# A seventh table of pairs and short slots for experts' last tokens

## The chip, the cores and the metric

The kernel runs on one core of one Trainium2 chip. The metric is the device time in microseconds (us) of one execution. The names PE, DVE, ACT, POOL and SP stand for the engines TensorE, VectorE, ScalarE, GpSimd and SyncE.

## What is computed

The reference has two halves. The first is a long convolution by Fourier transform, whose result multiplies the input; it gives 45824 rows (tokens) of 128 numbers. The second is a mixture of experts over these rows:

```
skip_score = x @ w_skip;  do_compute = skip_score > 0
out = x.copy();  xc = x[do_compute]
logits = xc @ w_gate                 # 8 experts
e_idx = argmax(logits);  gate_w = softmax(logits)[e_idx]
for e in range(8):                   # F = 1024
    h = relu(xc[e_idx == e] @ w1[e])            # 128 -> 1024
    y[e_idx == e] = gate_w * (h @ w2[e])        # 1024 -> 128
out[do_compute] = xc + y
```

The inputs are drawn with a fixed seed. Counted with the reference, 22861 tokens are computed, and the eight experts get 2546, 2933, 2278, 3602, 2666, 2440, 2962 and 3434 of them. In blocks of 256 that is 93 blocks, the last of each expert partly filled: with 242, 117, 230, 18, 106, 136, 146 and 106 tokens.

## The kernel before, in words

Three stages run one after the other: the first transforms and the filter (to about 350 us), the product in frequency and the way back (to about 900 us), and the output stage, which makes the rows, routes each token to its expert and stores all rows to memory. The output stage works in 32 chunks of 128 x 12 rows. For each chunk it appends the tokens' row numbers to lists, one list per expert.

An expert's tokens are computed in **slots** of 256 (`T`). A **table** decides which experts' blocks fill the next slots. `KNOWN` lists the tables: `(c, n, u)` says that after chunk `c` a table fills `n` units of `u` slots each. With `u` = 2, a **pair**, both slots belong to one expert, so that they share its weights. Before, six tables give 72 slots. The first 28 (`NEARLY`) run beside the output stage (`early_slots`), 44 as 22 pairs after it. A table after the last chunk (`last`) gives `NLAST` = 21 single slots. What is left over runs in a loop whose count is known at run time only (L919; it starts at `NLAST`). `table` (L535) is a generator: its small DVE operations and small PE products on 8 numbers are spread over the steps of the output stage, at two points of each step (`tabled`).

The code of each step is written in a fixed order, and each engine takes its instructions in that order. The early slots are a second generator (`work`): one piece of it goes into each step, and `PACE` - 1 more pieces per step on average. What remains of it follows the last step.

`late_slots` (L802) then goes through its units `u`. For a unit it gathers the rows four units ahead (`fetch`, L643 on POOL, one indirect DMA for 128 rows), turns them (PE transposes into `mtp`, L695), splits them and the weights into a high and a low part (L697 and L701, L678 and L683), and makes each product as three fp32r products (L706 to L708 for the first product `up`, L839 to L841 for `down`). ACT and DVE take the first product through relu as a high and a low part (L827, L828). The down product has the 128 features on the partitions, so its result is copied (`yt`, L845, once per unit, on ACT), transposed back (`mto`, L852), weighted and added on DVE (L719) and stored by POOL (L712, one indirect DMA for 128 rows). After each unit's gathers and after its stores POOL writes a small tile (`idle`, L616). The down product of unit `u` - 1 stands between the up products of unit `u`.

Of the kernel before, what the change touches and what calls it, by code (L numbers as in the profile page):

```python
# [39 lines left out]

KNOWN = ((3, 4, 1), (5, 4, 1), (9, 3, 2), (14, 7, 2), (23, 12, 2), (29, 10, 2))
SOON = 4
# [6 lines left out]
QX = 4  # L49
PACE = 1.3  # L50
START = (0, 4, 7)
# [7 lines left out]
FETCH = 4  # L59
NLATE = 65  # L60
NLAST = NEARLY + NLATE - NKNOWN
NTAB = 188
IDLE = 512
FRONT = 7


def units():

    at, found = 0, []
    for n, u in [(n, u) for _, n, u in KNOWN] + [(NLAST, 1)]:  # L70
        found += [list(range(k, k + u)) for k in range(at, at + n * u, u)]
        at += n * u
    return [v for v in found if v[0] < NEARLY], [v for v in found if v[0] >= NEARLY]

# [406 lines left out]
class Experts:  # L481
# [7 lines left out]
    def __init__(self, tc, i, out, lists, mc, wf):  # L489
# [28 lines left out]
        nc.vector.memset(self.found, 0.0)  # L518
        self.tab = mc.tile([1, NKNOWN + NTAB], I32, name="tab")
        self.addr = mc.tile([1, NKNOWN + NTAB], I32, name="addr")  # L520
        self.total = mc.tile([1, 1], I32, name="total")
        self.ids = mc.tile([128, NKNOWN + NLAST, 2], I32, name="ids")
        self.flat = lists.rearrange("a b -> (a b)")
# [10 lines left out]

    def table(self, last, base, limit, unit, pool, ps):  # L535

# [3 lines left out]
        mm = nc.tensor.matmul  # L540
        col = lambda name, dt=F32: pool.tile([E, 1], dt, name=name)
        shift, incl = self.shift[:, 0], self.shift[:, 1]
        done, iota = self.done, self.iota[:, 0:limit]
        ni, nt, cum, step = col("tni", I32), col("tnt", F16), col("tcum"), col("tstep")
# [16 lines left out]

        past = pool.tile([E, NTAB], F32, name="past", bufs=1)[:, 0:limit]
        pasth = pool.tile([E, NTAB], F16, name="tph", bufs=1)[:, 0:limit]
        nc.vector.tensor_scalar(past, iota, cum, None, ALU.is_ge)
# [6 lines left out]
        yield  # L571
        at = pool.tile([1, NTAB], F32, name="trow", bufs=1)[:, 0:limit]
        nc.vector.scalar_tensor_tensor(at, iota[0:1], float(T * unit), r, ALU.mult, ALU.add)
# [5 lines left out]
        if not last:  # L579

            dn = col("tdn")
# [20 lines left out]
    def fetch(self, at, ids, since):  # L602
        at = self.nc.sync.value_load(at, min_val=0, max_val=END)
        ins = self.nc.sync.dma_start(ids, self.flat[ds(at, T)].rearrange("(p a) -> p a", a=2))
        self.group(ins, "fetches", *(f"list{c}" for c in self.listed if c > since))

    def issue(self, s, ch):
        self.fetch(self.addr[:, s:s + 1], self.ids[:, s], ch)

# [192 lines left out]
    def late_slots(self, pool):  # L802
# [4 lines left out]
        with (  # L807
# [40 lines left out]
            def leave(sts, yt):  # L848
# [9 lines left out]
                self.rest()  # L858

            self.apart = False  # L860
            st, w, h = self.ahead
# [3 lines left out]
            def fetch(u):  # L865
                if u < count:
                    for n in UNITS[u]:
                        if n not in st:
                            st[n] = self.gather(n, self.ids[:, n], pool, self.names[n])
# [4 lines left out]
            sts = lambda u: [st[n] for n in UNITS[u]]  # L874
            w2, yt = {}, {}
            before = iter(())
            for u in range(count + 2):
                fetch(u + FETCH)
                if u + 1 < count:
                    hl[u + 1] = turned(sts(u + 1))  # L880

                def first():
                    if u + 1 < count:
                        w1[u + 1] = self.split(st[UNITS[u + 1][0]][0], pool, 0, nc.vector)
# [4 lines left out]
                def finish():  # L889
                    if u >= 2:  # L890
                        leave(sts(u - 2), yt.pop(u - 2))

                def lower():
                    y = next(before, None)
                    if y is not None:
                        yt[u - 1] = y
                parts = []
                if u >= count:
                    finish()
                elif len(UNITS[u]) == 1:  # L900
                    first()
                    hp = up(w1[u], hl[u], 0)
                    finish()
                    parts.append(relu(hp))
                    second()
                    parts.append(relu(up(w1[u], hl[u], 1)))
                else:
                    for k, rest in enumerate((finish, first, second, lambda: None)):
                        hp = up(w1[u], hl[u], k)
                        lower()  # L910
                        parts.append(relu(hp))
                        rest()
                while u >= 1 and u - 1 < count and u - 1 not in yt:
                    lower()
                if u < count:
                    before = down(w2[u], parts, hl[u].shape[2])
                    del w1[u], hl[u]
# [37 lines left out]
def out_phase(tc, i, out, zd, ex, consts):  # L955
# [6 lines left out]
    with (  # L962
        tc.tile_pool(name="slot", bufs=2, reuse_waits="tile") as eb,
    ):
      with (
# [237 lines left out]
        groups = [(s, ch, b) for ch, (b, n, u) in checks.items() for s in range(b, b + n * u)]  # L1203
        groups += [(s, NCH - 1, NKNOWN) for s in range(NKNOWN, NKNOWN + NLAST)]
        fresh = []

# [25 lines left out]
        def routed(ch):  # L1232
            route(ch)
            last = ch == NCH - 1
            if last or ch in checks:
                span = (NKNOWN, NTAB, 1) if last else checks[ch]
                tables.append(ex.table(last, *span, ob, tabs))

# [139 lines left out]
```

## Time and profile before

| | us |
|---|---|
| median of 3 runs | 1631.91 |
| the three runs | 1627.84, 1638.36, 1631.91 |
| the profiled execution's own time | 1634.26 |
| its span, first to last instruction | 1632.5 |

The profile is of one execution. Over the whole span PE is busy for 95%, DVE for 73%, POOL for 67% and ACT for 49%; PE alone holds 79% of the chain of work that ended last. The output stage ends near 1213 us; from there to the end only expert slots run. Lines (L845) are those of the kernel before; in the changed kernel the same lines stand 14 to 70 further down. Matmuls overlap one another in the records, so the distance from one start to the next is the time that one takes.

### The profile page before, as it was taken

The numbers are of one execution on the slowest core, as the hardware profiler recorded it, in microseconds if no ns is written. First come the engines' busy times: TensorE is split into PE (matmuls) and PEld (weight loads), VectorE is DVE, ScalarE is ACT, GpSimd is POOL, SyncE is SP. The second block draws the span as 40 slices with busy tenths as digits, with TensorE's granted clock in tenths as the row PEclk, the third lists the DMA queues.
The fourth block names the chain that finished last, engine by engine and source line by source line (L and its number), as shares of the span: only waits on it lengthen the run. The fifth ranks groups of instructions, "written<-read, shape, count | busy, mean of one in ns | idle before, by whom it ended". The sixth has DMA issues, their size and how long they took to land.

```text
span 1632.5 us, 26515 instructions
## 1 busy us (share of the span) xinstructions
PE 1542.9 (95%) x8272; PEld 965.3 (59%) x8272; DVE 1198.7 (73%) x2403; ACT 795.1 (49%) x1691; POOL 1099.1 (67%) x857
## 2 busy tenths in 40 slices
PE   8976999999999999988889999999989999998997
PEld 3542444444444444433467766666778877888997
DVE  2325877888788799985878777777867776776886
ACT  5543545445444444433344453443545554555764
POOL 1103898888988788850474749656687876766885
PEclk9897999999999999999899999999999999999999
DMA  9998999999999789969967778769321111111110
GB/s 324 325 340 313 383 378 377 352 331 317 341 338 330 246 263 334 290 195 338 308 207 241 252 237 244 244 213 286 104 43 42 44 45 39 44 35 35 34 34 21
DMA packets 200644, 361.92 MB, mean 222 GB/s; under 512 B 64842, under 2 KB 141018, under 8 KB 200462
## 3 DMA queue, kind: packets, MB, share of 16 engines
q1 hardware_dynamic: 181078, 316.98, 57.3%
q0 software_dynamic: 16704, 38.89, 8.4%
q10 hardware_dynamic: 2720, 4.34, 0.9%
q8 instruction: 67, 1.10, 0.3%
q14 instruction: 75, 0.61, 0.1%
HBM read 216.96 MB, written 145.69 MB: 222 GB/s over the span
## 4 chain that ended last, share of the span: by engine, by line
PE 79%; DVE 7%; issue 6%; DMA 4%; ACT 1%; POOL 1%; SPq 0%; another core or an unknown queue 0%; DVEq 0%; ACTq 0%; POOLq 0%
PE ps L405 19%; PE xp L374 12%; PE bank L789 6%; PE ps L203 4%; PE y L1031 4%; PE hp L706 4%; PE hp L708 4%; PE my L841 4%; PE my L839 4%; PE my L840 4%; PE hp L707 4%; PE tp L1044 2%; PE mh L706 2%; PE bank L1052 1%; DMA x1f<-fx 1%
## 5 line engine op out<-in xcount | busy, mean ns | idle before, releaser
L405 PE MATMUL ps<-y,c 128*128 128x512 f32 x720 | 331.3, 597 | 0.3
L472 POOL TENSOR_TENSOR y<-y,p 128x2048 f32<-128x2048 f32 x59 | 267.6, 4535 | 68.7 <-DVE p L394 68.7
L712 POOL DMA_INDIRECT out<-o,ids x186 | 205.5, 1105 | 151.1 <-DVE o L719 110.6
L405 PEld LDWEIGHTS ps<-y,c 128*128 128x128 f32 x720 | 133.4, 190 | 173.0 <-issue 155.7
L643 POOL DMA_INDIRECT xt<-out,ids x186 | 197.4, 1061 | 50.8 <-issue 32.5
L394 DVE TENSOR_TENSOR p<-xp,g 128x1024 f32<-128x1024 f32 x240 | 217.4, 948 | 0.0
L828 DVE SCALAR_TENSOR_TENSOR hh<-hp,hh 128x1024 fp32r<-128x1024 f32 x130 | 158.4, 1218 | 76.5 <-ACT hh L827 47.5
L394 DVE TENSOR_TENSOR y<-xp,g 128x1536 f32<-128x1536 f32 x120 | 210.8, 1757 | 4.0
L406 ACT COPY z<-ps 128x512 f32<-128x512 f32 x180 | 105.5, 586 | 178.5 <-PE ps L405 164.5
L827 ACT ACTIVATE hh<-hp 128x1024 fp32r<-128x1024 f32 x130 | 134.2, 1032 | 86.7 <-PE hp L708 52.0
L473 POOL TENSOR_TENSOR y<-y,p 128x1024 f32<-128x1024 f32 x59 | 139.0, 2356 | 4.6
L683 DVE TENSOR_TENSOR ws<-wf,ws 128x1024 fp32r<-128x1024 f32 x104 | 126.6, 1217 | 12.7 <-ACT ws L678 9.9
L616 POOL MEMSET idle<- 128x512 f16 x248 | 134.5, 542 | 0.2
L706 PE MATMUL hp<-hl,ws 128*128 128x512 f32 (+1 forms) x344 | 124.4, 362 | 7.5 <-DVE hh L828 5.2
L203 PE MATMUL ps<-wf,c 60*120 60x384 f32 x512 | 113.4, 535 | 12.1 <-DVE wf L186 11.4
L1031 PE MATMUL y<-zt,c 128*64 128x512 f32 x384 | 110.9, 647 | 14.0 <-DVE xm L1032 8.0
L789 PEld LDWEIGHTS bank<-wd,h 128*128 128x128 f32 x896 | 105.5, 194 | 29.6 <-issue 29.6
L374 PE MATMUL xp<-x,wf 128*128 128x480 f32 x256 | 115.5, 575 | 7.3 <-issue 3.5
L205 ACT COPY wf<-ps 120x384 f32<-120x384 f32 x256 | 105.6, 493 | 26.7 <-PE ps L203 25.9
L707 PE MATMUL hp<-hl,ws 128*128 128x512 f32 (+1 forms) x344 | 116.7, 339 | 1.0 <-issue 1.0
L841 PE MATMUL my<-hh,ws 128*128 128x512 f32 (+1 forms) x344 | 117.2, 341 | 0.4 <-issue 0.4
L839 PE MATMUL my<-hh,ws 128*128 128x512 f32 (+1 forms) x344 | 117.2, 341 | 0.0
(165 smaller groups left out, 3003.5 us busy)
## 6 DMA issues: line engine op xcount, KB each, us to landing
wf<-xv SPq DMA_DIRECT2D x64, 768.0 KB
x1d<-wf SPq DMA_DIRECT2D x64, 720.0 KB
x<-x1d SPq DMA_DIRECT2D x60, 768.0 KB
zt<-zd SPq DMA_DIRECT2D x60, 768.0 KB
zd<-z SPq DMA_DIRECT2D x110, 384.0 KB
out<-xm SPq DMA_DIRECT2D x96, 258.0 KB
ox<-xo SPq DMA_DIRECT2D x96, 256.0 KB
x1f<-fx POOLq DMA_DIRECT2D x16, 720.0 KB
```

The costliest lines, as they stand in the source:

```text
L203: nc.tensor.matmul(ps[p], self.c1[rows], u[rows, q * RUN:(q + 1) * RUN], start=True, stop=True)
L374: nc.tensor.matmul(xp[:, k, 0:(NS + NB) * DH], c2(n % PER * KS + j * KH + k), x1[:, j * KH + k], start=True, stop=True)
L394: nc.vector.tensor_tensor(o[:, :, :, j * KH:(j + 1) * KH].rearrange("p s a k b d -> p (s a) k b d"), x[:, None].broadcast_to([128, m, KH, ...
L405: nc.tensor.matmul(zps, c3[:, a, :], y[:, blk, a], start=(a == 0), stop=(a == 1))
L472: nc.gpsimd.tensor_tensor(y[:, 1:], y[:, 1:], p1, ALU.add)
L643: ins = nc.gpsimd.indirect_dma_start(out=xt[:, j], out_offset=None, in_=self.rows[0:have], in_offset=bass.IndirectOffsetOnAxis(ap=ids[:, j ...
L706: nc.tensor.matmul(hp, w[:, 0, c], hl[:, 0], start=True, stop=False)
L707: nc.tensor.matmul(hp, w[:, 0, c], hl[:, 1], start=False, stop=False)
L712: ins = nc.gpsimd.indirect_dma_start(out=self.rows, out_offset=bass.IndirectOffsetOnAxis(ap=ids[:, j:j + 1], axis=0), in_=o, in_offset=Non ...
L789: nc.tensor.matmul(bank[:, j * D:(j + 1) * D], h[f][:, j * 128:(j + 1) * 128], wd[s][:, f * D:(f + 1) * D], start=(f == 0), stop=(f == F / ...
L839: nc.tensor.matmul(y, w2[:, 0, c], h[:, 0], start=(f == 0), stop=False)
L841: nc.tensor.matmul(y, w2[:, 1, c], h[:, 0], start=False, stop=(f == F // 128 - 1))
```

## The change

The seven steps of it: a table of 7 pairs after chunk 32 is added to `KNOWN`; `NLAST` falls from 21 to 3 (28 + 61 - 86); four short slots (`NHALF`) are added at the end; the last table of pairs counts a block as full when it holds more than 128 tokens (`most`); a new table (`half`) finds the experts whose last block has 1 to 128 tokens and takes that block out of `found`; `PACE` goes from 1.3 to 1.24; and `late_slots` gets a short form for the short slots. That form gathers 128 rows, transposes once, copies the weights once instead of splitting them, uses one plain fp32 product instead of three fp32r ones, does relu on ACT alone, and makes the down product with the tokens on the partitions, so that `yt` and the transpose back fall away.

```
-KNOWN = ((3, 4, 1), (5, 4, 1), (9, 3, 2), (14, 7, 2), (23, 12, 2), (29, 10, 2))
+KNOWN = ((3, 4, 1), (5, 4, 1), (9, 3, 2), (14, 7, 2), (23, 12, 2), (29, 10, 2), (32, 7, 2))
-PACE = 1.3
+PACE = 1.24
-NLATE = 65
+NLATE = 61
+NHALF = 4
+HALF = NKNOWN + NTAB
...
+    found += [[HALF + k] for k in range(NHALF)]
...
-    def table(self, last, base, limit, unit, pool, ps):
+    def table(self, kind, base, limit, unit, pool, ps):
...
+        half, last = kind == "half", kind == "last"
...
-        nc.vector.tensor_scalar(ni, self.found, float(T - 1 if last else 0), None, ALU.add)
-        nc.vector.tensor_scalar(ni, ni, 8, None, ALU.arith_shift_right)
+        def rounded(n, up):
+            nc.vector.tensor_scalar(n, self.found, float(up), None, ALU.add)
+            nc.vector.tensor_scalar(n, n, 8, None, ALU.arith_shift_right)
+        rounded(ni, {"full": 0, "most": T // 2 - 1, "half": T - 1, "last": T - 1}[kind])
+        if half:
+            done, nw = col("done", F16), col("nw", I32)
+            rounded(nw, T // 2 - 1)
+            nc.vector.tensor_copy(done, nw)
...
-            nc.vector.scalar_tensor_tensor(done, dn, float(unit), done, ALU.mult, ALU.add)
+            if half:
+                nc.vector.scalar_tensor_tensor(self.found, dn, float(-T), self.found, ALU.mult, ALU.add)
+            else:
+                nc.vector.scalar_tensor_tensor(done, dn, float(unit), done, ALU.mult, ALU.add)
...
-        for j in range(2):
+        for j in range(ids.shape[1]):
...
+            def turned_half(st):
+                tp = mpt.tile([128, 2 * T], F32, name="mtp")[:, 0:128]
+                nc.tensor.transpose(tp, st[1][:, 0, 0:D], self.ident)
+                x = pool.tile([128, 2, 2 * T], F32R, name="hl", bufs=2)[:, 0, 0:128].bitcast(F32)
+                nc.scalar.copy(x, tp)
+                return x
+
+            def weight_half(st, which, p, eng):
+                w = p.tile([128, 2, F], F32R, name=f"ws{which}", bufs=2)[:, 0].bitcast(F32)
+                src = (self.w1f, self.w2f)[which][:, ds(self.where(eng, st[0]), F)]
+                (eng.copy if eng is nc.scalar else eng.tensor_copy)(w, src)
+                return w
+
+            def up_half(w, x):
+                hp = mph.tile([128, 4 * T], F32, name="hp")
+                for f in range(F // 128):
+                    c = slice(f * 128, (f + 1) * 128)
+                    nc.tensor.matmul(hp[:, c], w[:, c], x, start=True, stop=True)
+                h = mb.tile([128, 2, 4 * T], F32R, name="hh", bufs=6)[:, 0].bitcast(F32)
+                nc.scalar.activation(h, hp, AF.Relu)
+                return h
+
+            def down_half(w, h):
+
+                y = mpy.tile([128, 2 * T], F32, name="my")[:, 0:D]
+                for f in range(F // 128):
+                    c = slice(f * 128, (f + 1) * 128)
+                    nc.tensor.matmul(y, h[:, c], w[:, c], start=(f == 0), stop=(f == F // 128 - 1))
+                yield y
+
+            def leave_half(st, y):
+                tb, xt, ids, since = st
+                o = self.row()
+                self.gated(o[:, 0, 0:D], y, xt, 0)
+                self.store(o[:, 0], ids, 0)
+                self.rest()
...
-                tables.append(ex.table(last, *span, ob, tabs))
+            if not last and ch in checks:
+                tables.append(ex.table("full", *checks[ch], ob, tabs))
+            if last:
+                tables.append(zip_longest(ex.table("most", *checks[ch], ob, tabs), ex.table("half", HALF, NHALF, 1, ob, tabs[:, 64:])))
+                tables.append(ex.table("last", NKNOWN, NTAB, 1, ob, tabs))
```

How the order of the instructions moves is shown at three places. The first is DVE after the last chunk's counts are in `found`. Before, three small operations of the table `last` follow `tf` (the tokens' places in their lists), and then the weighting of an early pair:

```order
L1158 CAST tf<-to 128x24
L545 TENSOR_SCALAR tni<-found 8x1
L546 TENSOR_SCALAR tni<-tni 8x1
L548 TENSOR_TENSOR tnt<-tni,done 8x1
L719 SCALAR_TENSOR_TENSOR o_4455<-bank_4479,xt_4451 128x128 x2
```

Now the tables `most` (t...) and `half` (h...) open with eleven:

```order
L1228 CAST tf<-to 128x24
L554 TENSOR_SCALAR tni<-found 8x1
L555 TENSOR_SCALAR tni<-tni 8x1
L564 TENSOR_TENSOR tni<-tni,done 8x1
L565 TENSOR_SCALAR tni<-tni 8x1
L566 CAST tnt<-tni 8x1
L554 TENSOR_SCALAR hni<-found 8x1
L555 TENSOR_SCALAR hni<-hni 8x1
L554 TENSOR_SCALAR hnw<-found 8x1
L555 TENSOR_SCALAR hnw<-hnw 8x1
L560 CAST hdone<-hnw 8x1
L562 TENSOR_TENSOR hnt<-hni,hdone 8x1
```

PE's first products of the table (on `tnt`, now also on `hnt`) wait for the last of them. The second place is PE a little later, where the table `last` now runs as a third one behind the other two, between groups of eight products of an early pair (L810, L789 before):

```order
L810 MATMUL bank_4479<-wd,h 128x128 x8
L568 LDWEIGHTS shift
L568 MATMUL bank_4478<-tnt,shift 8x1
L569 LDWEIGHTS shift
L569 MATMUL bank_4478<-done,shift 8x1
L810 MATMUL bank_4479<-wd,h 128x128 x8
L582 LDWEIGHTS onesf
L582 MATMUL bank_4478<-tph,onesf 1x188
L583 MATMUL bank_4478<-tpast,tstep 1x188
L584 LDWEIGHTS done
L584 MATMUL bank_4478<-first,done 1x188
L810 MATMUL bank_4479<-wd,h 128x128 x8
```

Before, this part of the program had one table with its products between pieces of early work, and no second one behind it. The third place is PE at the very end, in the short slots (`xt_4448` and `xt_4449` are the rows of the last two, `mto` belongs to the last single slot):

```order
L883 MATMUL mtp<-ident,xt_4448 128x128
L898 MATMUL hp<-hl,ws_17864 128x128 x8
L908 MATMUL my<-ws_17853,hh 128x128 x8
L873 MATMUL mto<-ident,yt 128x128 x2
L883 MATMUL mtp<-ident,xt_4449 128x128
L898 MATMUL hp<-hl,ws_17940 128x128 x8
L908 MATMUL my<-ws_17929,hh 128x128 x8
L898 MATMUL hp<-hl,ws_18003 128x128 x8
L908 MATMUL my<-ws_17992,hh 128x128 x8
L908 MATMUL my<-ws_18039,hh 128x128 x8
```

Where a single slot had 48 products of 256 columns and four transposes, a short one has 16 products of 128 columns and one transpose.

## Rows read from the trace of the kernel before

**Rows 1.** The head of the page.
```profile
span 1632.5 us, 26515 instructions
```

**Rows 2.** Windows: output stage, its end, pairs, single slots; busy us of each engine.
```profile
core 0: us, PE busy (x) PEld busy (x) DVE busy (x) ACT busy (x) POOL busy (x), PEclk, DMA share, GB/s
900.00:1150.00 250.00, 245.85 (x2057) 168.15 (x2055) 194.28 (x687) 114.23 (x286) 164.34 (x194) 1.00 0.78 247
1150.00:1213.00 63.00, 57.57 (x457) 45.72 (x455) 44.57 (x171) 25.26 (x52) 45.69 (x54) 0.97 0.26 64
1213.00:1484.00 271.00, 264.14 (x1239) 216.77 (x1240) 195.41 (x280) 152.34 (x179) 203.07 (x213) 0.99 0.16 41
1484.00:1622.00 138.00, 131.70 (x1066) 129.29 (x1064) 111.09 (x157) 89.89 (x119) 105.73 (x113) 0.98 0.12 31
```

**Rows 3.** Timeline of ACT, the copy that ends a unit: start us, us, line.
```profile
1228.60 0.58 ACT L845 COPY yt<-my 128x512 f32<-128x512 f32 x1 [2.13 <-PE my L841]
...
1450.48 0.59 ACT L845 COPY yt<-my 128x512 f32<-128x512 f32 x1 [2.12 <-PE my L841]
1462.30 0.59 ACT L845 COPY yt<-my 128x512 f32<-128x512 f32 x1 [2.12 <-PE my L841]
...
1490.42 0.37 ACT L845 COPY yt<-my 128x256 f32<-128x256 f32 x1 [1.58 <-issue]
...
1606.35 0.37 ACT L845 COPY yt<-my 128x256 f32<-128x256 f32 x1 [1.53 <-PE my L841]
1612.53 0.38 ACT L845 COPY yt<-my 128x256 f32<-128x256 f32 x1 [1.52 <-PE my L841]
1618.49 0.37 ACT L845 COPY yt<-my 128x256 f32<-128x256 f32 x1 [1.69 <-PE my L841]
1622.31 0.37 ACT L845 COPY yt<-my 128x256 f32<-128x256 f32 x1 [3.45 <-issue]
```

**Rows 4.** Timeline of ACT, 1369 us: a late start within the pairs.
```profile
1369.34 1.02 ACT L827 ACTIVATE hh<-hp 128x1024 fp32r<-128x1024 f32 x1 [5.18 <-PE hp L708]
```

**Rows 5.** Timeline of PE: plain fp32 products of 128 columns, 64 together.
```profile
1202.21 7.31 PE L789 MATMUL bank<-wd,h 128*128 128x128 f32 x64
```

**Rows 6.** Lines, each form apart, 1213 to 1622 us: busy us, mean ns.
```profile
L712 POOL DMA_INDIRECT out<-o,ids x130 | 146.7, 1128 | 72.5 <-DVE o L719 42.0 <-issue 25.0 <-DVE hh L828 2.1
L827 ACT ACTIVATE hh<-hp 128x1024 fp32r<-128x1024 f32 x129 | 133.1, 1032 | 80.2 <-PE hp L708 45.5 <-issue 20.6 <-PE mtp L695 5.6
...
L683 DVE TENSOR_TENSOR ws<-wf,ws 128x1024 fp32r<-128x1024 f32 x85 | 103.4, 1217 | 11.4 <-ACT ws L678 9.9 <-DVE hl L701 0.8 <-issue 0.7
L678 ACT CAST ws<-wf 128x1024 fp32r x85 | 88.5, 1042 | 2.9 <-issue 2.3
...
L616 POOL MEMSET idle<- 128x512 f16 x85 | 46.1, 543 | 0.0
L719 DVE SCALAR_TENSOR_TENSOR o<-mto,xt 128x128 f32<-128x128 f32 x128 | 36.5, 337 | 4.8 <-PE hp L708 2.8 <-PE mto L852 1.9
```

**Rows 7.** The same view of the whole run: a copy of 128 columns on ACT.
```profile
L1054 ACT COPY lt<-bank 128x128 f32<-128x128 f32 x96 | 26.0, 271 | 21.7 <-PE bank L1052 19.9 <-PE bank L1144 0.5
```

**Rows 8.** Timeline of POOL at the end.
```profile
1623.84 0.97 POOL L712 DMA_INDIRECT out<-o,ids  x1 [1.03 <-DVE o L719]
1625.12 0.97 POOL L712 DMA_INDIRECT out<-o,ids  x1 [0.30 <-issue]
1626.09 0.54 POOL L616 MEMSET idle<- 128x512 f16 x1
```

**Rows 9.** Timeline of DVE: ten small operations of a table, first and last.
```profile
1164.38 0.15 DVE L573 SCALAR_TENSOR_TENSOR trow<-iota,bank 1x10 f32<-1x10 f32 x1
...
1165.58 0.15 DVE L586 SCALAR_TENSOR_TENSOR done<-tdn,done 8x1 f16<-8x1 f32 x1
```

**Rows 10.** Windows: ten us near the end of the output stage.
```profile
1180.00:1190.00 10.00, 7.34 (x65) 6.86 (x64) 8.63 (x30) 0.96 (x4) 6.84 (x8) 0.89 0.43 107
```

**Rows 11.** Waits of PE, 1150 to 1213 us: us in total, times, longest.
```profile
PE bank L1121 <- DVE ct L1112: 2.1, 1, 2.1
```

More of the change, by code (lines that the diff above doesn't have):

```diff
@@ L1 @@
+from itertools import zip_longest
 import numpy as np
@@ L518, in __init__ @@
         nc.vector.memset(self.found, 0.0)
-        self.tab = mc.tile([1, NKNOWN + NTAB], I32, name="tab")
-        self.addr = mc.tile([1, NKNOWN + NTAB], I32, name="addr")
+        self.tab = mc.tile([1, HALF + NHALF], I32, name="tab")
+        self.addr = mc.tile([1, HALF + NHALF], I32, name="addr")
         self.total = mc.tile([1, 1], I32, name="total")
-        self.ids = mc.tile([128, NKNOWN + NLAST, 2], I32, name="ids")
+        self.ids = mc.tile([128, NKNOWN + NLAST + NHALF, 2], I32, name="ids")
         self.flat = lists.rearrange("a b -> (a b)")
@@ L533, in weights @@
                           i["moe_w2"][e].rearrange("(c p) d -> p c d", p=128))
-    def table(self, last, base, limit, unit, pool, ps):
+    def table(self, kind, base, limit, unit, pool, ps):
         nc = self.nc
         mm = nc.tensor.matmul
-        col = lambda name, dt=F32: pool.tile([E, 1], dt, name=name)
+        half, last = kind == "half", kind == "last"
+        pre, room = ("h", limit) if half else ("t", NTAB)
+        col = lambda name, dt=F32: pool.tile([E, 1], dt, name=pre + name)
         shift, incl = self.shift[:, 0], self.shift[:, 1]
         done, iota = self.done, self.iota[:, 0:limit]
-        ni, nt, cum, step = col("tni", I32), col("tnt", F16), col("tcum"), col("tstep")
-        nc.vector.tensor_scalar(ni, self.found, float(T - 1 if last else 0), None, ALU.add)
-        nc.vector.tensor_scalar(ni, ni, 8, None, ALU.arith_shift_right)
+        ni, nt, cum, step = col("ni", I32), col("nt", F16), col("cum"), col("step")
+        def rounded(n, up):
[6 more added lines that the diff above has]
+            nc.vector.tensor_copy(done, nw)
         if unit == 1:
@@ L559, in table @@
         nc.vector.scalar_tensor_tensor(step, nt, float(-T * unit), step, ALU.mult, ALU.add)
-        past = pool.tile([E, NTAB], F32, name="past", bufs=1)[:, 0:limit]
-        pasth = pool.tile([E, NTAB], F16, name="tph", bufs=1)[:, 0:limit]
+        past = pool.tile([E, room], F32, name=pre + "past", bufs=1)[:, 0:limit]
+        pasth = pool.tile([E, room], F16, name=pre + "ph", bufs=1)[:, 0:limit]
         nc.vector.tensor_scalar(past, iota, cum, None, ALU.is_ge)
@@ L571, in table @@
         yield
-        at = pool.tile([1, NTAB], F32, name="trow", bufs=1)[:, 0:limit]
+        at = pool.tile([1, room], F32, name=pre + "row", bufs=1)[:, 0:limit]
         nc.vector.scalar_tensor_tensor(at, iota[0:1], float(T * unit), r, ALU.mult, ALU.add)
@@ L579, in table @@
         if not last:
-            dn = col("tdn")
+            dn = col("dn")
             nc.vector.tensor_tensor(dn, cum, nt, ALU.subtract)
@@ L603, in fetch, with listing @@
         at = self.nc.sync.value_load(at, min_val=0, max_val=END)
-        ins = self.nc.sync.dma_start(ids, self.flat[ds(at, T)].rearrange("(p a) -> p a", a=2))
+        a = ids.shape[1]
+        ins = self.nc.sync.dma_start(ids, self.flat[ds(at, 128 * a)].rearrange("(p a) -> p a", a=a))
         self.group(ins, "fetches", *(f"list{c}" for c in self.listed if c > since))
     def issue(self, s, ch):
-        self.fetch(self.addr[:, s:s + 1], self.ids[:, s], ch)
+        self.fetch(self.addr[:, s:s + 1], self.listing(s), ch)
+    def listing(self, s):
+        return self.ids[:, s] if s < HALF else self.ids[:, s - NTAB + NLAST, 0:1]
     def pause(self):
@@ L868, in fetch @@
                         if n not in st:
-                            st[n] = self.gather(n, self.ids[:, n], pool, self.names[n])
+                            st[n] = self.gather(n, self.listing(n), pool, self.names[n])
                             if n == UNITS[u][-1]:
@@ L874, in late_slots @@
             sts = lambda u: [st[n] for n in UNITS[u]]
+            part = lambda u: UNITS[u][0] >= HALF
             w2, yt = {}, {}
@@ L879, in late_slots @@
                 if u + 1 < count:
-                    hl[u + 1] = turned(sts(u + 1))
+                    hl[u + 1] = turned_half(*sts(u + 1)) if part(u + 1) else turned(sts(u + 1))
                 def first():
-                    if u + 1 < count:
+                    if u + 1 < count and part(u + 1):
+                        w1[u + 1] = weight_half(*sts(u + 1), 0, pool, nc.scalar)
+                    elif u + 1 < count:
                         w1[u + 1] = self.split(st[UNITS[u + 1][0]][0], pool, 0, nc.vector)
@@ L889, in finish @@
                 def finish():
-                    if u >= 2:
+                    if u >= 2 and not part(u - 2):
                         leave(sts(u - 2), yt.pop(u - 2))
@@ L896, in lower @@
                         yt[u - 1] = y
+                        if part(u - 1):
+                            leave_half(*sts(u - 1), y)
                 parts = []
                 if u >= count:
+                    lower()
+                    finish()
+                elif part(u):
+                    w2[u] = weight_half(*sts(u), 1, mb, nc.vector)
+                    first()
+                    parts = up_half(w1[u], hl[u])
+                    lower()
                     finish()
@@ L915, in late_slots @@
                 if u < count:
-                    before = down(w2[u], parts, hl[u].shape[2])
+                    before = down_half(w2[u], parts) if part(u) else down(w2[u], parts, hl[u].shape[2])
                     del w1[u], hl[u]
@@ L1204, in out_phase @@
         groups += [(s, NCH - 1, NKNOWN) for s in range(NKNOWN, NKNOWN + NLAST)]
+        groups += [(HALF + k, NCH - 1, HALF) for k in range(NHALF)]
         fresh = []
```

2 lines of the change are left out of this document (removed).

## The prediction, made before the changed kernel ran

> **What bounds the kernel now.** I read the windows by stage first [rows 2]. From 900 to 1150 us PE is busy for 245.85 of 250 us; from 1150 to 1213, where the routing of the last chunks runs dry, it stands idle for 5.4 of 63 us; among the pairs (to 1484) for 6.9 of 271 and among the single slots (to 1622) for 6.3 of 138. So PE sets the time in all stages that the change touches, and what counts is how much PE work goes and how much PE idleness comes. POOL, at 203 of 271 us, is the next.
>
> What one unit costs is read from the copies that end a unit [rows 3], not from busy sums, because matmuls overlap. Undisturbed, a pair takes 1462.30 - 1450.48 = 11.82 us and a single slot 1612.53 - 1606.35 = 6.18 us. Averaged, a pair takes (1462.30 - 1228.60) / 19 = 12.30 us and a single slot (1618.49 - 1490.42) / 19 = 6.74 us. The difference is late starts such as that of ACT at 1369.34, 5.18 us idle although its product had been ready for most of that [rows 4]; the profile names no cause for them. Per us they are denser among the singles (9%) than among the pairs (4%).
>
> **The change, part by part.**
>
> *Units.* 14 of the 21 singles become 7 pairs, 4 become short slots, 3 stay. That the 3 and 4 suffice follows from the counted tokens: with the last blocks of 117, 18, 106 and 106 tokens made short, 89 full blocks remain, 72 of them placed by the first six tables; stepping the tables through the counted tokens chunk by chunk leaves seven pairs and 3 single blocks. Seven more pairs cost 7 x 12.30 = 86.1 us (undisturbed 82.7), 18 fewer singles save 18 x 6.74 = 121.3 us (undisturbed 111.2) [rows 3]. Together -35.2 by averages, -28.5 undisturbed. I take the averages: fewer instructions should meet fewer late starts.
>
> *Short slots.* Price per slot by engine. PE: 64 products of the same kind and size took 7.31 us, 0.114 us each [rows 5]; 16 of them and a transpose make 1.9 us. ACT: a copy of 128 columns 0.27 [rows 7], weights 1.04, relu 1.03 [rows 6], together 2.34 us. DVE: no row shows its plain copy of 128x1024; its two-operand form took 1.22 [rows 6], and nothing makes a copy dearer than that, so with the weighting (0.34) at most 1.6 us. Even that upper end lies beside ACT's 2.34, so I cost it at nothing; with ACT's work gone it would be next behind PE. POOL: one store 1.13 and the small tile 0.54 [rows 6], with gaps about 1.9 us. By itself ACT would set the pace; but at the end POOL is queued up, since the last single slot's two stores (2 x 1.13 + 0.30 + 0.54, about 3.3 us with a gap) stand between the stores of the first and the second short slot.
>
> The row against which a rule must be held is that of the plain fp32 product [rows 5]. The Trainium skill, page "FP8 and Floating Point Precision", section "TensorE Precision Notes", says that true fp32 takes four passes through the array; at 2.4 GHz four passes of 128 columns would be an estimated 0.213 us a product, 3.4 us a short slot, and the four slots would cost some 5 us more than I count. The trace, with 0.114 us, doesn't agree for this form.
>
> *The end.* Before, from the last unit's copy to the end of the span are 1632.5 - 1622.31 = 10.2 us [rows 1, 3]; of this 5.9 us follow POOL's last instruction [rows 1, 8], and that stays. Now, from the copy of the last single slot: transpose, up and down of the next 2.0 us, weighting and issue 0.7, then POOL in a row 1.9 + 3.3 + 1.9 + 1.9 + 1.7 = 10.7, then 5.9: 19.3 us, 9.1 more. Bounds: if POOL weren't in the way, ACT's pace gives 3 x 2.34 + 0.9 + 0.7 + 1.7 + 5.9 = 16.2 (6 more); if PE fell to half its clock or needed four passes, 3.7 us a slot gives about 21.3 (11 more). I take 9, since POOL's rows are of the same instructions.
>
> *Late stage:* -35.2 + 9 = -26.2 us. Bounds: -19.5, if as much time is lost in late starts as before where the removed units stood (-28.5 + 9), and -29.6, if the new pairs meet none (82.7 - 121.3 + 9).
>
> *Tables.* DVE gets some 38 small operations more after the last chunk. Ten of them took 1.35 us [rows 9], so they are some 6 us of DVE in all. Three places put them before PE. First, eleven instead of three stand before the first table products: 8 x 0.135 = 1.1 us later, while the cover falls from 16 products of an early pair (16 x 0.114 = 1.8 us) to six fp32r products of 512 columns, 1.5 us at most (a pair has 48 of them, 11.82 / 48 = 0.246 each). About 1.4 us of PE idle. Second, the third table waits for the 18 operations that close the other two (2.4 us), for the split of an early pair's weights (1.22, [rows 6]) and of its rows, and three more of its own: about 5 us against 2.5 us of PE work. About 2.5 us idle. Third, its second products wait some 0.5 us. Against these 4.4 us: in the trace DVE's split stands before the last chunk's counts, and PE waits 2.1 us for them [rows 11]; in the new order that split stands behind, so most of this wait goes; and of the 5.4 us idle in this stretch [rows 2] another part was in the places just priced. `PACE` 1.24 leaves about 12 fp32r products and 32 early down products more behind the last chunk's counts, some 7 us that now cover; PE's sum of work is the same, and before 1150 us PE has little idle time to give back. I take +2 us. Bounds: -3 (the 2.1 us and a little more go, the rest is covered) and +8 (nothing is covered, and the clock falls: where PE was idle for 2.7 of 10 us the granted clock was 0.89 [rows 10], a part of the time at 1.2 GHz instead of 2.4).
>
> *Queues.* POOL: four gathers, four stores and 17 small tiles fewer; its cycle in a pair (4 stores, 4 gathers, two tiles) fits into 11.82 us before, and the seven new pairs are like the old ones. SP: 93 list fetches before and after, the new ones more than 200 us before their use. Nothing added waits there.
>
> **Sum:** 1634.26 - 26.2 + 2 = 1610.1 us for an execution like the profiled one. That execution lies 2.35 us above the median of the three, 1631.91; on the median's level I forecast **1608 us**.
>
> **The rivals.**
>
> A. *The tables' chain is laid bare.* PE idles at each of the three places, with a low clock behind it: +8 instead of +2, 1614 us, and with the bound of +10 1616. For it: 38 DVE operations in series and DVE busy for 8.6 of 10 us there [rows 10]. Against: about 7 us of early work more behind them.
>
> B. *Plain fp32 costs four passes, or the thin products drop the clock:* 11 instead of 9 at the end, and up to 2 us more before it: 1610 to 1612. This is the page's rule, told above. Against: 0.114 us a product [rows 5]. For a low clock: short slots fill PE for 1.9 of 2.34 us at best.
>
> C. *The late starts go with the singles:* -29.6 and the tables at -3, 1600 us. For it: they are densest among the singles. Against: they occur among pairs too, up to 6 us [rows 3, 4].
>
> D. *Slower: the run-time loop runs.* Place: the loop behind the late slots, which starts at 3 now. If the short slots' blocks weren't taken out of `found`, or the pairs' parities left more, the last table counts more than 3. One pass has nothing beside it: two gathers 2.1, weights 1.04 + 1.22, one relu in two parts 1.03 + 1.22, two stores 2.3, a tile 0.5 and the 48 products of a single slot (5.8 of its 6.18) are 15.2 us at least, without the landing of list and rows. From the third pass on it decides: 1608 + 46 = 1654 us; with all four short blocks counted again 1669. Against: the counted tokens give exactly 3 and 4, none of the last blocks nearer to 128 than 8 tokens, and the loop didn't run before either. It is also the case in which the change doesn't do what it says.
>
> **How the numbers follow.** Forecast 0.66 (1603 to 1614), A 0.12, B 0.09, C 0.10, D 0.03. The range runs from C with the lowest run's distance below the median (4 us, the three runs span 10.5) cut by half, 1598, to the forecast with late starts as dense as before and the tables' upper part, 1634.26 - 19.5 + 7 - 2.35 = 1619. One per cent, about what a measurement of this kernel can tell from no change, puts the border at 1615.6 us. Faster: nearly all of the forecast, B and C and half of A, 0.87. Slower: D, 0.03, of which a part would still be within. The rest, within 1%: 0.11; I give 0.86, 0.11 and 0.03.
>
> **What would show it.** In the changed profile: 29 unit copies of 512 columns and 3 of 256, with 12.0 to 12.3 us from pair to pair; the copy of the last single about 19 us before the end; plain fp32 products 0.11 to 0.12 us apart in the short slots; POOL's last stores in a row without a wait for DVE; PE idle for 5 to 9 us between 1150 us and the first late products. Wrong would be: a pass of the loop (gathers after the last short slot's store), short slots more than 3 us apart on ACT, or an output stage that ends more than 8 us later.

## The result and the profile after

The changed kernel takes 1615.21 us (median of 4 runs, 1611.32 to 1615.95); the kernel before takes 1631.47 us beside it (4 runs, 1627.84 to 1638.36). The ratio is 0.9891, interval 0.9865 to 0.9917: faster by about 1.1%, 16.3 us, where 24 were forecast. The profiled execution took 1615.34 us.

The page's head, and the windows of the four stages as in [rows 2]:
```profile
span 1613.5 us, 25463 instructions
...
900.00:1150.00 250.00, 246.42 (x2081) 168.75 (x2079) 197.67 (x701) 114.04 (x290) 159.12 (x189) 0.99 0.79 245
1150.00:1213.00 63.00, 56.67 (x421) 45.55 (x421) 43.55 (x180) 25.35 (x47) 46.00 (x57) 0.92 0.26 63
1213.00:1484.00 271.00, 261.00 (x1200) 211.94 (x1199) 190.70 (x278) 149.03 (x173) 208.74 (x215) 0.99 0.16 42
1484.00:1613.00 129.00, 122.03 (x705) 106.15 (x703) 84.24 (x126) 71.00 (x87) 86.75 (x93) 0.99 0.12 32
```
PE is idle for 6.3 us where the tables stand (5.4 before), and for 10 of 271 us among the pairs (6.9 before). So the pairs, which the change leaves alone, got worse in this execution.

The copies that end a unit, as in [rows 3] (L866 is what L845 was):
```profile
1231.78 0.59 ACT L866 COPY yt<-my 128x512 f32<-128x512 f32 x1 [2.12 <-PE my L862]
...
1452.10 0.59 ACT L866 COPY yt<-my 128x512 f32<-128x512 f32 x1 [1.79 <-PE mtp L716]
1471.08 0.59 ACT L866 COPY yt<-my 128x512 f32<-128x512 f32 x1 [1.08 <-remote]
...
1576.44 0.59 ACT L866 COPY yt<-my 128x512 f32<-128x512 f32 x1 [4.44 <-PE my L862]
1583.07 0.37 ACT L866 COPY yt<-my 128x256 f32<-128x256 f32 x1 [1.67 <-PE mtp L883]
1590.71 0.37 ACT L866 COPY yt<-my 128x256 f32<-128x256 f32 x1 [0.68 <-remote]
1593.96 0.37 ACT L866 COPY yt<-my 128x256 f32<-128x256 f32 x1 [0.38 <-PE my L862]
```
The first late copy comes 3.2 us later than before. From it to the end there are now 1613.5 - 1231.78 = 381.7 us, against 403.9: 22.2 us less. One pair took 18.98 us, with two late starts in it, as in [rows 4]:
```profile
1460.91 1.02 ACT L848 ACTIVATE hh<-hp 128x1024 fp32r<-128x1024 f32 x1 [5.57 <-remote]
...
1468.04 1.02 ACT L848 ACTIVATE hh<-hp 128x1024 fp32r<-128x1024 f32 x1 [5.18 <-PE mtp L716]
```

The short slots on PE and on the engines beside it (timeline from the second slot's up products on):
```profile
1597.71 1.95 PE L898 MATMUL hp<-hl,ws 128*128 128x128 f32 x16
...
1598.22 0.98 POOL L733 DMA_INDIRECT out<-o,ids  x1 [2.24 <-DVE o L740]
...
1598.86 0.85 DVE L891 COPY ws<-wf 128x1024 f32 x1 [0.23 <-DVE o L740]
1599.20 0.97 POOL L637 MEMSET idle<- 128x512 f16 x1
...
1599.50 1.95 PE L908 MATMUL my<-ws,hh 128*128 128x128 f32 x16
...
1601.29 1.95 PE L898 MATMUL hp<-hl,ws 128*128 128x128 f32 x16
...
1603.07 3.74 PE L908 MATMUL my<-ws,hh 128*128 128x128 f32 x32
...
1605.69 0.98 POOL L733 DMA_INDIRECT out<-o,ids  x1 [0.44 <-DVE o L740]
...
1606.85 0.35 DVE L740 SCALAR_TENSOR_TENSOR o<-my,xt 128x128 f32<-128x128 f32 x1 [1.44 <-PE my L908]
```
PE runs without a gap: eight products in `up_half` show as 16 records, and the next group starts 1.78 us later. A short slot's two groups are thus 3.56 us of PE, not 1.9. The last stores on POOL wait for DVE, and DVE for PE. But POOL is not far behind: from 1598.22 to 1605.25 us its stores and tiles follow one another with gaps of 0.17 to 0.30 us.

### The profile page after: what moved, and what is told of

Read it like the earlier page. It is cut to its first block, busy times and chain, and to the rows that moved or that the text cites. A ratio compares the mean times of both kernels' runs of the same rounds, so it can differ in the third digit from the quotient of the medians.

```text
span 1613.5 us, 25463 instructions
## 1 busy us (share of the span) xinstructions
PE 1529.5 (95%) x7872; PEld 936.4 (58%) x7872; DVE 1167.9 (72%) x2401; ACT 773.6 (48%) x1651; POOL 1079.0 (67%) x832
## 5 line engine op out<-in xcount | busy, mean ns | idle before, releaser
L733 POOL DMA_INDIRECT out<-o,ids x182 | 198.4, 1090 | 129.8 <-DVE o L740 88.0
L664 POOL DMA_INDIRECT xt<-out,ids x182 | 192.8, 1059 | 61.8 <-issue 32.0
L849 DVE SCALAR_TENSOR_TENSOR hh<-hp,hh 128x1024 fp32r<-128x1024 f32 x122 | 148.7, 1219 | 100.6 <-ACT hh L848 78.4
L848 ACT ACTIVATE hh<-hp 128x1024 fp32r<-128x1024 f32 x122 | 126.2, 1035 | 107.6 <-PE hp L729 54.2
L637 POOL MEMSET idle<- 128x512 f16 x231 | 126.2, 546 | 0.3
L208 PE MATMUL ps<-wf,c 60*120 60x384 f32 x512 | 111.1, 531 | 14.1 <-DVE wf L191 14.1
L1101 PE MATMUL y<-zt,c 128*64 128x512 f32 x384 | 109.5, 635 | 13.3 <-DVE xm L1102 5.1
L810 PEld LDWEIGHTS bank<-wd,h 128*128 128x128 f32 x896 | 103.9, 192 | 31.1 <-issue 31.1
L727 PE MATMUL hp<-hl,ws 128*128 128x512 f32 (+1 forms) x256 | 104.2, 407 | 10.8 <-issue 4.1
L191 POOL TENSOR_TENSOR wf<-wf 124x768 f32<-124x768 f32 x45 | 81.9, 1821 | 47.4 <-DMA wf<-xv 37.1
L810 PE MATMUL bank<-wd,h 128*128 128x128 f32 x896 | 113.7, 281 | 0.0
L704 DVE TENSOR_TENSOR ws<-wf,ws 128x1024 fp32r<-128x1024 f32 x82 | 101.3, 1235 | 2.8 <-issue 1.2
L391 DVE TENSOR_TENSOR g<-xp,g 128x128 f32<-128x128 f32 x120 | 34.7, 289 | 93.9 <-ACT g L384 93.8
```

What stands on the lines that cost most here:

```text
L208: nc.tensor.matmul(ps[p], self.c1[rows], u[rows, q * RUN:(q + 1) * RUN], start=True, stop=True)
L637: self.nc.gpsimd.memset(self.idle, 0.0)
L664: ins = nc.gpsimd.indirect_dma_start(out=xt[:, j], out_offset=None, in_=self.rows[0:have], in_offset=bass.IndirectOffsetOnAxis(ap=ids[:, j ...
L733: ins = nc.gpsimd.indirect_dma_start(out=self.rows, out_offset=bass.IndirectOffsetOnAxis(ap=ids[:, j:j + 1], axis=0), in_=o, in_offset=Non ...
L810: nc.tensor.matmul(bank[:, j * D:(j + 1) * D], h[f][:, j * 128:(j + 1) * 128], wd[s][:, f * D:(f + 1) * D], start=(f == 0), stop=(f == F / ...
L848: nc.scalar.activation(h[:, 0], hp, AF.Relu)
```

## The experiments

Four chips were used: A for the result above, then B, C and D, one for each group of runs below. The kernel before takes 1631.5 us on A and 1614.0, 1612.6 and 1614.6 us on B, C and D. Expectations were written before each group.

**The changed kernel again (B).** No edit.

> The changed kernel once more, to see whether its late starts stand still. In the profile taken first, units 7, 8 and 19 of the late pairs took 13.6, 14.1 and 19.0 us instead of 11.86. If a late start belongs to a place in the program, the same units are long again, and the first 20 pairs end some 5.6 us later than before in every execution. If it is chance, other units are long, and the time from the first to the twentieth pair differs by several us from 239.3.

1599.9 us (1596.69 to 1600.35), ratio 0.991 [0.9892, 0.9929]. No late start is left:
```profile
1231.26 0.59 ACT L866 COPY yt<-my 128x512 f32<-128x512 f32 x1 [2.13 <-PE my L862]
...
1567.59 0.38 ACT L866 COPY yt<-my 128x256 f32<-128x256 f32 x1 [1.75 <-PE my L862]
1573.67 0.37 ACT L866 COPY yt<-my 128x256 f32<-128x256 f32 x1 [1.50 <-PE my L862]
1578.65 0.37 ACT L866 COPY yt<-my 128x256 f32<-128x256 f32 x1 [2.12 <-PE my L862]
```
From pair to pair it is 11.85 to 11.86 us until the last full pairs; from the first late copy to the end (1598.2 us) 366.9 us, 14.8 less than on A with the same program.

**The kernel before again (C).** No edit.

> The kernel before once more, for a second trace of it. If the late starts are a matter of the single execution or the chip, its pairs take 11.83 us and its singles 6.18 throughout wherever the changed kernel's do, its first late copy comes near 1228.6 us and the span is near 1613. If they belong to places in its program, the pair that took 18.2 us and the single that took 12.5 are long again.

1615.48 us, span 1613.7.
```profile
1229.60 0.59 ACT L845 COPY yt<-my 128x512 f32<-128x512 f32 x1 [2.12 <-PE my L841]
...
1593.80 0.38 ACT L845 COPY yt<-my 128x256 f32<-128x256 f32 x1 [1.53 <-PE my L841]
1599.76 0.37 ACT L845 COPY yt<-my 128x256 f32<-128x256 f32 x1 [1.69 <-PE my L841]
1603.58 0.37 ACT L845 COPY yt<-my 128x256 f32<-128x256 f32 x1 [3.45 <-PE my L841]
```
Pairs are 11.82 to 11.87 us apart, singles 6.18: the late stage takes 384.1 us, against 403.9 on A. So late starts belong to the chip or the execution, not to places in the program. For the chip speaks that every run on A was longer than every run elsewhere: the kernel before took 1627.84 us or more there and 1618.85 or less on the others, the changed kernel 1611.32 or more and 1605.74 or less. With the two undisturbed traces the stage's undisturbed gain is 384.1 - 366.9 = 17.2 us.

**Only the seventh table of pairs (B).** Eight pairs, no short slots:
```
-(29, 10, 2), (32, 7, 2))          +(29, 10, 2), (32, 8, 2))
-NLATE = 61                        +NLATE = 65
-NHALF = 4                         +NHALF = 0
-"most": T // 2 - 1                +"most": T - 1
-tables.append(zip_longest(most, half))   +tables.append(most)
```


> Only the table of pairs: 8 pairs after the last chunk, partly filled blocks among them, 5 single slots, no short slots. By undisturbed periods 8 pairs for 16 singles save 16 x 6.18 - 8 x 11.82 = 4.3 us, and the second table in a row costs 2 us: -2 us, ratio 0.998 to 0.999. By averaged periods, with the late starts of the singles gone, 16 x 6.74 - 8 x 12.30 = 9.4 us less 2: -7 us, ratio 0.9955.

1613.56 us, ratio 1.0001 [0.9988, 1.0015]. The late stage is 379.8 us, 4.3 less than undisturbed before (8 x (11.85 - 2 x 6.18) = -4.1), and in the time nothing of it can be told from noise. The trace shows a part of the loss ahead of the tables: the output stage began at 734.3 us, where the two profiles of the kernel before have 731.4 and 732.5, and it lasted 497.4 us to the first late copy, as long as before. That 2 to 3 us may be an offset of the program as built; see the last group of runs.
```profile
L1101 PEld LDWEIGHTS y<-zt,c x384: 132/136/232, 734.3 to 1152.6; 128*64 128x64 f32 x192
```

**Only the short slots (B).** Without the seventh table of pairs: 17 singles and 4 short slots.
```
-(29, 10, 2), (32, 7, 2))                 +(29, 10, 2))
-tables.append(zip_longest(most, half))   +tables.append(half)
```


> Only the short slots: no seventh table of pairs, 17 single slots, then 4 short ones. By undisturbed periods 4 singles save 24.7 us, the end after the last single's copy is 19.5 instead of 10.2 us, the last single's period 0.6 us shorter, the tables cost 2 us: -14 us, ratio 0.9915. By averaged periods -16.5 us, 0.990. If the pairs' table were where the gain comes from, under 8 us: above 0.995. Short slots bound by PE show plain fp32 products 0.22 us apart and POOL waiting for DVE; bound by POOL's queue, stores without such waits.

1602.68 us, ratio 0.9929 [0.9912, 0.9945]. The late stage is 370.1 us, 14.0 less than undisturbed before. The short slots carry the gain. The whole change is 2.8 us faster still by the medians, 3.2 us by the late stage, but the intervals of the two ratios overlap.

**`PACE` 1.3 (B) and 1.18 (C).** `-PACE = 1.24`, `+PACE = 1.3` and `+PACE = 1.18`.

> The changed kernel with PACE back at 1.3. If the early work that the lower pace leaves behind is what covers the tables, the first late copy comes 2 to 5 us later than the 1231.8 us of the changed kernel, and the ratio to the kernel before rises from 0.989 to 0.991 or 0.993. If PE only has the same work in another order, nothing moves by more than 1 us: 0.989.

> The changed kernel with PACE 1.18, so that still less early work stands ahead of the tables. From 1.30 to 1.24 the first late copy came 2.9 us earlier. If more early work behind the last chunk's counts keeps covering the tables' waits, it comes another 1 to 2.5 us earlier, near 1229 to 1230 us, and the ratio is 0.990 or a little under the changed kernel's. If the waits that are left don't depend on how much work stands behind them (the DVE chain ahead of the first products of a table), nothing moves by more than 1 us.

1.3: 1603.35 us, ratio 0.9928 [0.9903, 0.9953], first late copy at 1234.12. 1.18: 1608.16 us, ratio 0.9969 [0.9954, 0.9984], first late copy at 1234.43, 505.6 us behind the start of the output stage, and 8.5 us instead of 4.5 between POOL's last instruction and the end. Of these 4 us, 3.3 lie in the longest DRAIN at POOL's end, and 0.8 in the INC_SWDGE_SEM ahead of it (1.30 us instead of 0.51). Both are instructions that close POOL's part of the program; why they are longer isn't shown. The DRAIN's shortest, median and longest time in ns, for the changed kernel on B and for 1.18:
```profile
L1447 POOLq DRAIN  x3: 46/103/1377, 1596.0 to 1597.9; - x3
```
```profile
L1447 POOLq DRAIN  x3: 46/103/4644, 1600.0 to 1605.2; - x3
```
Neither is better than 1.24; that 1.3 is worse lies within what the stage varies by (below). That early work left behind by a lower pace covers the tables is not shown by either run.

**One fp32r product in the short slots (C).** It leaves out the low parts of rows, weights and relu.
```
-... name="hl", bufs=2)[:, 0, 0:128].bitcast(F32)     +... [:, 0, 0:128]
-... name=f"ws{which}", bufs=2)[:, 0].bitcast(F32)    +... [:, 0]
-... name="hh", bufs=6)[:, 0].bitcast(F32)            +... [:, 0]
```


> The short slots with fp32r products in the place of the plain fp32 ones; the low parts are left out. If a plain fp32 product takes twice an fp32r one of 128 columns and PE sets the short slots' pace, a short slot falls from 3.7 us to ACT's pace of about 2.4, the time from the last single's copy to the end from 19.5 to 14.5 or 15.5 us, and the whole by 5 to 6 us. If POOL's queue of stores sets the end, as the prediction had it, the end moves by under 1 us.

1597.25 us, ratio 0.9889 [0.9853, 0.9925]; from the first late copy (1233.07) to the end 363.3 us, 3.6 less than with plain products, where 5 to 6 were expected. One line's instructions (median and range in ns, first and last start), first of the changed kernel on B, then of this one:
```profile
L898 PE MATMUL hp<-hl,ws x64: 273/275/275, 1573.5 to 1587.7; 128*128 128x128 f32 x64
```
```profile
L898 PE MATMUL hp<-hl,ws x32: 272/275/329, 1575.3 to 1584.3; 128*128 128x128 f32 x32
```
Both programs have 4 x 8 = 32 products there: a plain fp32 product leaves two records, an fp32r product one. The end of this kernel's POOL timeline:
```profile
1587.07 0.97 POOL L733 DMA_INDIRECT out<-o,ids  x1 [0.17 <-issue]
1588.04 0.54 POOL L637 MEMSET idle<- 128x512 f16 x1
1588.75 0.97 POOL L733 DMA_INDIRECT out<-o,ids  x1 [0.17 <-issue]
1589.72 0.54 POOL L637 MEMSET idle<- 128x512 f16 x1
1590.43 0.98 POOL L733 DMA_INDIRECT out<-o,ids  x1 [0.17 <-issue]
```
With cheap products the stores do stand in a row on POOL, without a wait for DVE: 16.8 us from the last single's copy to the end instead of 19.55. So POOL's row is the next limit behind PE, and that is why less was gained than expected.

**No small tile behind a short slot's store (C).** `-self.rest()` in `leave_half`.

> The changed kernel without POOL's small tile after each short slot's store. If PE sets the end, only the last tile counts: 0.5 us off the 19.5 from the last single's copy to the end. If POOL's queue sets it, four tiles with their gaps go: 2.6 us less, 16.9.

1599.09 us, one run; 1597.3 - 1578.21 = 19.1 us from the last single's copy to the end, 0.4 to 0.5 less. POOL now waits 1.88 us for DVE ahead of the last store but one, where it waited 0.44 us with the tiles, and the end comes earlier by no more than the last tile:
```profile
1578.21 0.37 ACT L866 COPY yt<-my 128x256 f32<-128x256 f32 x1 [2.12 <-PE my L862]
```
```profile
1589.94 0.97 POOL L733 DMA_INDIRECT out<-o,ids  x1 [1.88 <-DVE o L740]
```
POOL's queue isn't what the end waits for.

**The tables' first operations ahead of the routing (D).** PE waits for the tables behind the last counts, and its clock falls in the same stretch. `shared` runs the half table one round behind the table of pairs:
```
+        def shared(most, half, last):
+            for turn in ((most,), (half,), (most,), (most,), (half, most), (most, half), (half,)):
+                for t in turn:
+                    next(t, None)
+                yield
+            next(half, None)
+            yield from last
...
-            route(ch)
+            if ch == NCH - 1:
+                tables.append(shared(...most..., ...half..., ...last...))
+                tabled(0)
+            route(ch)
```


> The last chunk's first table operations (five on VectorE) stand ahead of that chunk's routing operations instead of behind them, and the short slots' table runs one round behind the pairs' table instead of beside it. Theory (the tables cost 2.7 to 3.2 us because TensorE waits for this chain, 1.9 + 0.65 us at about 1179 us, and the granted clock then falls to 0.75 between 1180 and 1190 us, which costs another 1.3 us): both waits go, the clock stays at 0.95 or more there, and the first late copy comes at 1228 to 1229.5 us instead of 1231.3; the kernel gains 2 to 3 us on the changed one, 1597 us on a chip where that one takes 1600. Rival (the time is given by the amount of VectorE work behind the last counts, not by its order): TensorE's waits move to the later products of the tables, the first late copy stays within 0.5 us of 1231.3, and the time is the same.

> As the kernel before it in this list, and without GpSimd's small tile behind each short slot's store. If TensorE sets the pace of the short slots: 0.4 to 0.5 us less from the last single slot's copy to the end, 19.1 instead of 19.55 us, as in the run that left out the tile alone, and together 2.5 to 3.5 us less than the changed kernel. If GpSimd's queue mattered: 2 us less in the end stage.

> The changed kernel again, beside the other two on the same chip. If the late starts belong to the chip and not to the program, its copies are 11.85 us apart through all pairs on a chip where the kernel before takes about 1613 us, and they are drawn out as in the first profile on one where it takes about 1630; ratio to the kernel before 0.989 to 0.993 in both cases.

| kernel (D) | median us | ratio to before |
|---|---|---|
| changed kernel again | 1598.73 (1596.57 to 1605.74) | 0.9908 [0.9887, 0.9929] |
| tables first | 1600.58 (1598.45 to 1603.58) | 0.9911 [0.9894, 0.9927] |
| tables first, no tile | 1594.94 (1594.41 to 1599.23) | 0.9882 [0.9864, 0.99] |

Waits of PE in the stretch of the tables, first of the changed kernel on A, as in [rows 11], then of the kernel with the tables first (1150 to 1225 us):
```profile
PE bank L1191 <- DVE nt L1180: 1.7, 1, 1.7
PE bank L568 <- DVE tni L565: 1.3, 1, 1.3
PE bank L568 <- DVE tnt L562: 0.9, 1, 0.9
...
PE bank L568 <- DVE hnt L562: 0.7, 1, 0.7
```
```profile
PE bank L1191 <- DVE ct L1182: 1.6, 1, 1.6
PE bank L1206 <- DVE sel L1220: 1.5, 3, 0.7
...
PE bank L568 <- DVE tnt L562: 1.1, 1, 1.1
PE bank L582 <- DVE hph L579: 1.0, 1, 1.0
PE bank L1246 <- DVE hstep L572: 0.9, 1, 0.9
```
The waits moved rather than went: the rival had that right. Of the 75 us from 1150 to 1225 PE is idle for 8.8 us with the tables first and 8.4 without the tile too, against 7.2 to 8.5 in the five executions of programs that are alike up to there (the changed kernel three times, one product, no tile). The clock didn't fall, though; its mean over these 75 us is 1.00 in both, against 0.93 to 0.98 in the five. Windows 1180 to 1190 us, first of the changed kernel on B, then with the tables first:
```profile
1180.00:1190.00 10.00, 8.18 (x57) 6.39 (x57) 7.37 (x47) 3.92 (x6) 8.46 (x11) 0.75 0.35 69
```
```profile
1180.00:1190.00 10.00, 8.74 (x65) 6.48 (x65) 8.73 (x45) 5.12 (x8) 9.12 (x11) 1.00 0.41 116
```
0.75 is half of the stretch at 1.2 GHz: products of 512 columns start 0.43 us apart there, with the tables first 0.23. But the waits for the tables, 1.91 and 0.65 us, don't come before the fall, as the expectation had it: on B the clock is 1.00 from 1170 to 1178 us and 0.51 from 1178 to 1185, and the first of these waits begins at 1179.2. Ahead of the fall PE had stood idle for 1.64 us, up to 1176.34; with the tables first it stands idle for 1.65 us at the same place and the clock stays. So why the clock fell isn't shown.

The first late copy itself is a poor measure of 2 us: in the five executions it stands at 1228.36 to 1233.07, and 497.6 to 502.0 us behind the start of the output stage (before: 497.2 and 497.1). From the weight load of the last `y` product (L1101) on it is steady:

| kernel | last `y` product to first late copy, us |
|---|---|
| before (A, C) | 70.8, 71.2 |
| `PACE` 1.3 | 74.6 |
| the five executions with all tables, `PACE` 1.24 | 81.7, 80.6, 81.3, 81.7, 80.6 |
| pairs' table alone; half table alone | 79.1; 79.1 |
| tables first; tables first, no tile | 79.3; 79.4 |

Two of its lines, of the changed kernel on D and of the kernel with the tables first, each with its first late copy:
```profile
L1101 PEld LDWEIGHTS y<-zt,c x384: 132/136/233, 730.8 to 1147.1; 128*64 128x64 f32 x192
```
```profile
1228.36 0.59 ACT L866 COPY yt<-my 128x512 f32<-128x512 f32 x1 [2.13 <-PE my L862]
```
```profile
L1101 PEld LDWEIGHTS y<-zt,c x384: 132/136/232, 735.1 to 1154.4; 128*64 128x64 f32 x192
```
```profile
1233.69 0.59 ACT L866 COPY yt<-my 128x512 f32<-128x512 f32 x1 [2.13 <-PE my L862]
```
The first two rows give the price of the tables at an equal pace, 3.4 to 3.8 us: in this stretch PE's work differs between them only by the tables' own small products. With 1.24 the stretch holds 24 more fp32r products of 512 columns and 4 more transposes, about 24 x 0.23 = 5.5 us and some 0.5, and it is 6.0 to 7.1 us longer, so as far as these rows show this work covers none of the tables' waits.

In this stretch the order gives back 1.8 of some 2 us that a second new table costs; since PE is idle as long as before, the clock is the part that changed (on B, PE was busy for 4.4 of the 7 us at the low level). For the whole output stage a gain isn't shown: from its start to the first late copy it lasts 498.6 and 496.4 us with the tables first, which the five, at 497.6 to 502.0, don't tell from chance. Nor does the whole time follow: the kernel with the tables first is no faster than the changed one, and there the output stage began at 735.1 us, in the two others on D at 730.8 and 730.2, ahead of all that the edits touch. Of the 3.8 us by which the last kernel is under the changed one, 1.8 and 0.5 are seen in the stretches edited (its end takes 19.0 us); the rest has no place there. With the tables first alone the median lies 1.8 us below the profiled execution, and in the kernel with the pairs' table alone at it, so a part of the late start may be an offset of the program as built; no run tested it. On D the changed kernel's pairs are 11.85 to 11.86 us apart until the last full ones, without a late start.

## Why the prediction came out as it did

The direction was right and the time lies in the range, 7 us above the forecast. The gain was 16.3 us on A, and 14.1 and 15.9 us on B and D, where 24 were forecast. By the steps, us:

| step | predicted | profiles on A | undisturbed (B, C, D; tables: all chips) |
|---|---|---|---|
| units and end, without late starts | -19.5 | | -17.2 |
| late starts | -6.7 | -5.0 | 0 |
| late stage | -26.2 | -22.2 | -17.2 |
| tables | +2 | +3.2 | +2.8 (mean of five, +0.4 to +4.9) |

*"I take the averages: fewer instructions should meet fewer late starts"* failed as a rule. On A the stage lost 403.9 - 384.1 = 19.8 us to them before and 381.7 - 366.9 = 14.8 after, so a part did go, 5.0 of the 6.7 forecast. But they don't belong to singles: before, the first 19 periods lost 233.7 - 224.8 = 8.9 us and the rest 10.9; after, the same 19 pairs lost 239.3 - 225.2 = 14.1, and all others under 1. On B, C and D none were there, and the same change brought 14 to 16 us by the medians. What causes them on A stays open. The Trainium skill, page "Runtime: NRT & Kernel Launch", section "Instruction fetch mechanics", says that a taken branch whose target isn't at hand stalls the engine for a fetch. The trace on A doesn't bear this out as the cause: ACT's first branch in this stage stands at 1603.7 us, and in the idle time ahead of the start at 1468.04 us no packet of an instruction queue moved at all.

*The price of a short slot on PE* was wrong by a factor of two, by a misread row. [rows 5] has 64 records, which I took for 64 products; they are 32. A plain product of 128 columns takes 1.78 / 8 = 0.223 us. I set the trace against the rule of four passes (the Trainium skill, page "FP8 and Floating Point Precision", section "TensorE Precision Notes"); its estimate, 0.213 us, agrees with the 0.223 us measured, and my reading was wrong. So PE, not ACT, sets the pace of the short slots, and relu on ACT comes 3.4 to 3.9 us apart (5.0 once, on B), over the 3 us that I named as a sign of error.

*The end* came out at 19.55 us, against 19.3, by errors that cancel, and that is luck: PE's slots were dearer, POOL's row wasn't the limit (the tiles' absence gave 0.4 to 0.5 us, where a row on POOL would have given 2.6), and 4.5 us, not 5.9, follow POOL's last instruction (its closing DRAIN took 1.38 us instead of 2.44; why isn't shown). The run with one product shows POOL's row as I described it, at 16.8 us. What the dear products cost ahead of the end I had not counted: the last two singles' periods are 6.07 + 4.99 us against 5.96 + 3.82, 1.3 us more. With 0.45 more at the end, and pairs at 11.855 instead of 11.83 us, that makes the 2.3 us between -19.5 and -17.2.

*The tables* came out at 3.4 to 3.8 us at an equal pace, against +2, and the terms behind the +2 were off both ways. The wait for the last counts, most of which was to go, fell only from 2.1 to 1.7 us. The second place cost 0.9 us instead of 2.5. The early work that `PACE` leaves behind was counted on as cover, and no run shows that it covers. The fall of the clock was in the upper bound, not in the +2.

The remaining 2 us are the level: before's profiled execution lies 2.8 us above its median, the changed kernel's on it. Rival B's mechanism, the dear plain product, was the true one; its price at the end was smaller than feared, 9.4 us instead of 11, of which 1.4 us are the shorter time behind POOL's last instruction. The clock didn't drop in the short slots (1.00 there). A's waits and low clock came at +3, not +8; C and D didn't occur.

## What to carry to other kernels

Before pricing an instruction from a row's count, check how many records one instruction leaves: products counted in the code against records of the same line. Where periods of equal units differ, take the undisturbed period for the change, and put the disturbance into the range. A gain of a few us is read from a distance between two near events in the trace, as here from the last `y` product, not from an absolute time that collects the variation of everything before it.

## What the runs showed of the hardware

- A plain fp32 product of 128x128 by 128 columns takes 0.223 us and leaves two matmul records; an fp32r product leaves one, and eight of them show 0.97 us of weight loads, which is (0.97 - 0.19) / 7 = 0.111 us from one to the next.
- VectorE's plain fp32 copy of 128x1024 took 0.69 us with no MEMSET beside it, and 0.85 us beside GpSimd's MEMSET, which then took 0.97 instead of 0.54 us.
- Late starts cost one chip 14.8 to 19.8 us of 400 in this stage, and three others nothing (traces of the changed kernel on two of them, of the kernel before on the third).
- Behind POOL's last instruction the span goes on for 4.5 to 8.6 us, and the difference lies in POOL's INC_SWDGE_SEM and closing DRAIN: 0.51 and 1.38 us in most builds, 0.79 and 2.44 in the kernel before, 1.30 and 4.64 with `PACE` 1.18.
